# Taking the scale of W_out from the greatest upper words as loaded, on VectorE, instead of from sums of squares on ScalarE

## The chip, the cores and the metric

The kernel runs on one core of a Trainium2 chip. Its time is the device time of one execution, in microseconds (us); the median of three runs is 661.01 us (660.56 to 662.23). The profiled execution, from which all rows below come, took 662.76 us, of which 661.0 us lie between its first and its last instruction (the span).

## What is computed

Attention with a decay over 8 batches, 8 heads, 576 positions and 64 columns a head, and on its result, as 4608 tokens of 512, one layer with a gate by softmax, a normalisation and two weight matrices. All inputs are float64.

```python
scores = scale * np.matmul(q, k.transpose(0, 1, 3, 2))
decay = cum[:, :, :, None] - cum[:, :, None, :]        # cum: running sum of log f
scores = np.where(causal, -1000000000.0, scores + decay)
attn = softmax(scores)
x = (attn @ v) as [4608, 512]
h = x @ w_in                                            # [512, 1024]
solu = h * softmax(h)
ln = (solu - mu) / np.sqrt(var + 1e-06) * g_ln
out = ln @ w_out                                        # [1024, 512]
```

## The kernel before

**Tiles.** Heads go in pairs, four pairs a batch, 32 in all (p from 0 to 31). The 576 queries of a pair are cut into five tiles (i from 0 to 4; 64 rows, then four of 128), and a tile of scores is as wide as its last key: 64, 192, 320, 448, 576. The first three tiles of a pair are its first half, the last two its second. `score_products` (lines 802 to 829) makes the scores in PSUM; `scores` (831) takes on VectorE the row minima nm and moves the scores to SBUF (line 846), on ScalarE the exponential with its sums (851), on POOL the sums' last touch (857), on VectorE the reciprocal ri (858), and then scales the weights. For batch 0, whose pairs are 0 to 3, POOL scales them (the helper's line 509), TensorE transposes them (898), ScalarE or VectorE copies them out as t_p (507, 509), and the products with v are in f32 (923). Later batches split into f16 upper and lower parts and transpose by DMA (516, 928). `values` ends with x_h on ScalarE (938) and x_l on VectorE (939): upper part and remainder of a layer's input. The layer over 128 tokens at a time (36 of them) has products with W_in (959 to 961), the softmax and normalisation (970 to 1006), and products with W_out (1029 to 1031), each matrix in an upper and a lower f16 part.

**W_out.** It comes as float64 in four quarters of 1 MB into two landing buffers by turns, t_raw (in a buffer that the transposed weights of the second half use later) and vraw of batch 1. `weights` (572) makes f32 of a quarter: ScalarE takes the upper words (line 586), POOL the top bits of the lower words (589), and VectorE joins them into wo_f (591). `prepare_w_out` (724) then has ScalarE square each of the quarter's two halves, times g and a small constant, with the sum of each row going into `tops["wo"]` (735 and 736; gs, made by POOL in line 568, holds g times the constant). `scale` (634) takes the greatest of the eight columns (640), turns it with TensorE (645), makes a power of two of it (`exponents`, 648), spreads it by TensorE (670) and reads it back (675, 676). `scale_w_out` (739) multiplies g by it into sg and makes the f16 parts (744 to 753). For W_in, `scale_w_in` (625) does otherwise: VectorE takes the greatest absolute value among the upper words as loaded, read as f32 (line 629), and `exponents` undoes the shift of the exponent (653, 654).

**Order.** Every piece of work is an `op` with an engine, a length and what it reads and writes. `Plan.schedule` (115) gives each op a rank, by its number in the table `RANK` (line 97: `o.due = RANK[o.seq]`), and lets each engine take, among the ops that are ready in the plan, the one of least rank. This sets the order of all five queues, and each engine takes its queue in order on the chip. Where the plan sees TensorE idle in its first 300 us, blank products of `ident` are written into TensorE's queue to the length of the gap (lines 1142 to 1155); they write to a bank that is free and are read by nobody.

```python
def share(t):
    return next((x for a, e, x in FILLED if a <= t / 1e3 < e), 0.0)
...
idle += [(x, k, int(share(t) * (y - x) / (256 * COLUMN))) for k, x, y in plan.spare(busy + 100.0, t)]
...
nc.tensor.matmul(dst[:, :256], blank[:, :P], blank, start=True, stop=True)
```

## Time and profile before

| | |
|---|---|
| median of the runs | 661.01 us |
| profiled execution | 662.76 us, span 661.0 us |
| TensorE (PE) | 632.1 us, 96% |
| VectorE (DVE) | 553.3 us, 84% |
| ScalarE (ACT) | 513.1 us, 78% |
| POOL | 399.8 us, 60% |
| DMA | 110.80 MB, mean 168 GB/s |
| blank products (line 1154) | 131 |

An engine's share is over the whole span. Where one engine has nearly no gaps, the time is what stands in its queue plus its gaps, and a row of the order of time names for each gap what ended it. The reader should keep apart the start (to about 55 us, in which batch 0 and the weights are prepared), the long middle, and the last 40 us, in which only the layer is left.

### The profile page before, as it was taken

The page shows a single profiled execution, that of the slowest core. Times are in us where ns is not written, and L with a number is a line of the kernel's source. Part 1 is how long each engine was busy: PE and PEld are TensorE (multiplying, and loading weights), DVE is VectorE, ACT ScalarE, POOL GpSimd, SP SyncE. Part 2 cuts the span into 40 slices and gives each one's busy share as a digit, 9 for nine tenths or more (in the row PEclk, how much of TensorE's full clock was granted, in tenths as well). Part 3 has the DMA queues.
Part 4 walks back from the last instruction along what each step waited for, and adds up shares of the span by engine and source line. Part 5 has one row for each costly group of instructions (what it writes and reads, how often), then busy time and mean ns, then how long its engine had stood idle before and what let it go on. Part 6 is the DMA issues. An engine that isn't in the chain of part 4 may idle for free. (4 is left out here: it accounts for less than half of the span.)

```text
span 661.0 us, 17338 instructions
## 1 busy us (share of the span) xinstructions
PE 632.1 (96%) x6305; PEld 345.3 (52%) x6305; DVE 553.3 (84%) x1644; ACT 513.1 (78%) x1290; POOL 399.8 (60%) x625
## 2 busy tenths in 40 slices
PE   5989999999999998989989999999999899999998
PEld 4666655554545545444545545445545455544445
DVE  6967999999999999999979989899899977983122
ACT  6899848978988897788877987987688679674333
POOL 3475851477766855768666756783787544667420
PEclk8999999999999999999999999999999999999999
DMA  8846118969899998999789899999849886887341
GB/s 333 330 168 223 57 53 216 169 108 235 166 183 202 197 204 150 189 200 214 182 156 214 145 199 218 178 183 189 137 85 179 130 150 101 148 156 139 75 96 48
DMA packets 262710, 110.80 MB, mean 168 GB/s; under 512 B 248288, under 2 KB 248736, under 8 KB 261600
## 3 DMA queue, kind: packets, MB, share of 16 engines
q1 hardware_dynamic: 262624, 109.69, 79.4%
q8 instruction: 49, 0.80, 0.5%
q14 instruction: 37, 0.30, 0.1%
HBM read 38.27 MB, written 9.66 MB: 73 GB/s over the span
## 5 line engine op out<-in xcount | busy, mean ns | idle before, releaser
L851 ACT ACTIVATE p<-p,nm 128x320 f32<-128x320 f32 (+4 forms) x208 | 133.0, 641 | 22.9 <-DVE nm L846 22.5
L825 PE MATMUL ps<-qk 64*128 64x288 f16 (+9 forms) x1056 | 104.2, 305 | 11.9 <-DMA qk<-in_qk_dram 5.8
L959 PE MATMUL hps<-wi_h,x_h 128*128 128x512 f16 x288 | 109.6, 381 | 1.8 <-DVE e L977 1.6
L857 POOL TENSOR_SCALAR sm<-sm 128x2 f32<-128x2 f32 (+1 forms) x128 | 36.6, 286 | 122.6 <-ACT p L851 80.1
L961 PE MATMUL hps<-wi_h,x_l 128*128 128x512 f16 x288 | 109.1, 379 | 0.0
L960 PE MATMUL hps<-wi_l,x_h 128*128 128x512 f16 x288 | 109.1, 379 | 0.0
L1029 PE MATMUL ps<-wo_f,zz 128*128 128x512 f16 x280 | 106.6, 381 | 0.0
L1031 PE MATMUL ps<-wo_f,zz 128*128 128x512 f16 x280 | 106.1, 379 | 0.0
L1030 PE MATMUL ps<-wo_f,zz 128*128 128x512 f16 x280 | 106.1, 379 | 0.0
L846 DVE CUSTOM_DVE_ANT_0 p<-ps,mask 128x320 f32<-128x320 f32 (+4 forms) x208 | 98.2, 495 | 2.7 <-POOL unscale L696 1.0
L879 DVE SCALAR_TENSOR_TENSOR wo_p<-p,ri,wo_p 128x448 f16<-128x448 f32 (+1 forms) x112 | 91.1, 838 | 2.6 <-ACT wo_p L507 1.9
L928 PEld LDWEIGHTS <-v 128*64 128x64 f16 x2520 | 70.8, 110 | 25.5 <-issue 22.3
L928 PE MATMUL ps<-t_p,v 128*64 128x128 f16 (+1 forms) x2520 | 79.7, 219 | 4.6 <-ACT y L1061 1.6
L1001 POOL TENSOR_TENSOR z<-e,z 128x1024 f16<-128x1024 f32 x32 | 71.7, 2240 | 20.0 <-ACT z L507 19.4
L970 DVE TENSOR_REDUCE st<-hps 128x1 f32<-128x1024 f32 x36 | 43.8, 1215 | 33.6 <-PE hps L961 33.5
L509 POOL TENSOR_SCALAR wo_p<-p,ri 128x576 f16<-128x576 f32 x56 | 50.9, 915 | 15.6 <-DVE ri L858 14.1
L973 ACT ACTIVATE e<-hps,st,unscale 128x1024 f32<-128x1024 f32 x32 | 38.4, 1199 | 23.9 <-DVE st L971 17.9
L977 DVE SCALAR_TENSOR_TENSOR e<-hps,e 128x1024 f32<-128x1024 f32 x36 | 43.9, 1219 | 11.6 <-ACT e L973 11.5
L825 PEld LDWEIGHTS <-qk 64*128 64x128 f16 x864 | 32.8, 94 | 38.4 <-issue 27.0
L823 PE MATMUL ps<-crow,pick 64*128 64x448 bf16 (+1 forms) x360 | 51.8, 276 | 0.0
L987 ACT ACTIVATE junk<-e,st 128x1024 bf16<-128x1024 f32 x36 | 41.2, 1146 | 9.6 <-DVE e L977 9.5
L959 PEld LDWEIGHTS <-x_h 128*128 128x128 f16 x288 | 28.1, 97 | 37.4 <-issue 8.3
(188 smaller groups left out, 1315.7 us busy)
## 6 DMA issues: line engine op xcount, KB each, us to landing
raws<-in_qk_dram SPq DMA_DIRECT2D x24, 576.0 KB, 5.0
vraw<-in_v_dram SPq DMA_DIRECT2D x8, 1280.0 KB, 7.7
out_dram<-y SPq DMA_DIRECT2D x35, 256.0 KB, 2.9
qk<-in_qk_dram SPq DMA_DIRECT2D x8, 576.0 KB, 9.2
wo_raw<-in_w_in_dram SPq DMA_DIRECT2D x4, 1024.0 KB, 8.3
t_raw<-in_w_out_dram SPq DMA_DIRECT2D x2, 1024.0 KB, 4.9
vraw<-in_w_out_dram SPq DMA_DIRECT2D x2, 1024.0 KB, 6.3
t_p<-p16s SPq DMA_TRANSPOSE x84, 3.4
```

The costliest lines, as they stand in the source:

```text
L825: nc.tensor.matmul(dst, x[row(h), 0, q0:q0 + P], y[row(h), 1, cols], start=(n == 0), stop=False)
L846: op(DVE, R_NS[i] if n == 0 else 442, at[i][h] + STEPS[0], lambda i=i, h=h, n=n, a=a, e=e, x=x, m0=m0: nc.vector.tensor_tensor_reduce(home ...
L851: op(ACT, E_NS[i] + (0 if banked(p, i) or i == 4 else 28), at[i][h] + STEPS[1], lambda i=i, h=h, x=x: nc.scalar.activation(home(i, h), hom ...
L879: op(DVE, L_NS[j], at[j][g] + STEPS[4], lambda j=j, g=g, nq=nq, h16=h16, l16=l16, r1=r1: nc.vector.scalar_tensor_tensor(l16(), home(j, g, ...
L928: nc.tensor.matmul(o[row(h), a:a + n], v16[m][:, x, 2 * j + h], t[:, y, i + j if h else i - j], start=(j == 0 and c == 0), stop=(j == i an ...
L959: nc.tensor.matmul(hps[:, sl], x_h, wi_h[:, c, sl], start=(c == 0), stop=False)
L960: nc.tensor.matmul(hps[:, sl], x_h, wi_l[:, c, sl], start=False, stop=False)
L961: nc.tensor.matmul(hps[:, sl], x_l, wi_h[:, c, sl], start=False, stop=(c == NCC - 1))
L1001: op(Z_LO[n], {DVE: 1280, POOL: 2130}[Z_LO[n]], at, lambda: engine(Z_LO[n]).tensor_tensor(z16[:, :, 1], e2, z16[:, :, 0], ALU.subtract), [ ...
L1029: nc.tensor.matmul(o, zz[:, a, 0, j], wo(0, k), start=(k == 0), stop=False)
L1030: nc.tensor.matmul(o, zz[:, a, 0, j], wo(1, k), start=False, stop=False)
L1031: nc.tensor.matmul(o, zz[:, a, 1, j], wo(0, k), start=False, stop=(k == NFC - 1))
```

## The change

The sums of squares go, and gs with them. In their place VectorE takes, for each quarter as it was loaded, the greatest absolute value of each half's upper words, read as f32 (the values of `tops["wo"]`, two columns for a quarter). When all four are there, three small steps on 128x8 undo the exponent's shift and multiply by g, the greatest is taken by its absolute value, and `exponents` treats "wo" like "wi" from there on. The table of ranks is another one: it has 3656 numbers in place of 3660, and nearly every number differs, mostly by a few places.

```diff
-    9, 12, 5, 26, 11, 15, 13, 14, 20, 46, 23, 21, 32, 51, 30, 35, 36, 37, 39, 44, 38, 43, 47, 1, 3, 7, 4, 8, 92, 162, 149, 166, 40, 172, 19, 24, 28,
...
-    gs, sg, ones = sb("gs", NFC), sb("sg", NFC), sb("ones", P, p=1)
+    sg, ones = sb("sg", NFC), sb("ones", P, p=1)
...
-    op(POOL, 200, -20, lambda: nc.gpsimd.tensor_scalar(gs, g_sb, SMALL, 1.0, ALU.mult, ALU.mult), [("g",)], [("gs",)])
...
-        op(DVE, 160, due, lambda: nc.vector.tensor_reduce(t[:, :, NFC:], t[:, :, :n], axis=AX.X, op=ALU.max),
+        op(DVE, 160, due, lambda: nc.vector.tensor_reduce(t[:, :, NFC:], t[:, :, :n], axis=AX.X, op=ALU.max, apply_absolute_value=x == "wo"),
...
-            if x == "wi":
-                nc.vector.tensor_scalar(f, f, 2.0 ** -112, None, ALU.mult)
-                nc.vector.tensor_scalar(bits, bits, 3, None, ALU.logical_shift_left)
+            if x in ("wi", "wo"):
+                if x == "wi":
+                    nc.vector.tensor_scalar(f, f, 2.0 ** -112, None, ALU.mult)
+                    nc.vector.tensor_scalar(bits, bits, 3, None, ALU.logical_shift_left)
                 nc.vector.tensor_scalar(f, f, 2.0 ** -40, None, ALU.max)
                 nc.vector.tensor_scalar(bits, bits, 0x7F800000, None, ALU.bitwise_and)
             else:
...
-        for k in (2 * c, 2 * c + 1):
-            op(ACT, 820, due, lambda k=k: nc.scalar.activation(
-                junk[:, :DM], w()[:, (k % 2) * DM:(k % 2 + 1) * DM], AF.Square, scale=gs[:, k:k + 1], accum_out=tops["wo"][:, 0, k:k + 1]),
-               [wk, ("gs",)], [("top", "wo", k)])
+        op(DVE, 1220, due, lambda: nc.vector.tensor_reduce(
+            tops["wo"][:, 0, 2 * c:2 * c + 2], now(t).rearrange("p c n -> p (c n)").bitcast(F32).rearrange("p (k n t) -> p k n t", k=2, t=2)[:, :, :, 1],
+            axis=AX.X, op=ALU.max, apply_absolute_value=True), tk, [("top", "wo", 2 * c), ("top", "wo", 2 * c + 1)])
 
     def scale_w_out(due):
+        tw = tops["wo"][:, 0, :NFC]
+
+        def values():
+
+            nc.vector.tensor_scalar(tw, tw, 2.0 ** -112, None, ALU.mult)
+            nc.vector.tensor_scalar(tw.bitcast(I32), tw.bitcast(I32), 3, None, ALU.logical_shift_left)
+            nc.vector.tensor_tensor(tw, tw, g_sb, ALU.mult)
+        op(DVE, 300, due, values, [("g",)], [("top", "wo", k) for k in range(NFC)])
         scale("wo", "wo", 0, 1, NFC, due)
```

**VectorE's queue, between the last row minima of the first halves and the first x_l.** Names: p_63 to p_67 are the score tiles of i from 0 to 4 (the same numbers in both), nm and ri the row minima and reciprocals, t_0_raw and vraw_77 the landing buffers of W_out's quarters; L846 becomes L853, L858 L865, L591 L590, L939 L946. Before:

```order
L858 RECIPROCAL ri_89<-sm_93 128x2
L846 ISA p_63,nm_88<-ps_150,mask 128x64
...
L858 RECIPROCAL ri_92<-sm_96 128x2
L846 ISA p_67,nm_85<-ps_148,mask 128x288
...
L846 ISA p_67,nm_85<-ps_147,mask,nm_85 128x288
L846 ISA nm_85 128x1
L858 RECIPROCAL ri_92<-sm_96 128x4
L939 SCALAR_TENSOR_TENSOR x_l<-ps_145,scale_117,x_h 128x320
L591 SCALAR_TENSOR_TENSOR wo_f_669<-wo_f_669,t_0_raw 128x1024
```

Now:

```order
L734 TENSOR_REDUCE top_wo<-t_0_raw 128x2
L865 RECIPROCAL ri_89<-sm_93 128x2
...
L734 TENSOR_REDUCE top_wo<-vraw_77 128x2
L853 ISA p_67,nm_85<-ps_148,mask 128x288
...
L853 ISA p_67,nm_85<-ps_149,mask,nm_85 128x288
L853 ISA nm_85 128x1
L590 SCALAR_TENSOR_TENSOR wo_f_648<-wo_f_648,t_0_raw 128x1024
L590 SCALAR_TENSOR_TENSOR wo_f_648<-wo_f_648,vraw_77 128x1024
L946 SCALAR_TENSOR_TENSOR x_l<-ps_145,scale_116,x_h 128x320
L865 RECIPROCAL ri_92<-sm_96 128x4
```

Two of the four reductions, and the first two joins of W_out, now stand ahead of the fourth pair's reciprocal of four columns (ri_92); before, only the row minima did. The other two reductions follow: one just ahead of the last x_l, the other behind the third join.

**TensorE's queue, up to the first layer product.** L898 (now L905) are transposes of weights, L923 (now L930) products with v of batch 0, L1154 (now L1161) the blank products, L959 (now L966) the first product with W_in. Before:

```order
L898 MATMUL ps_148<-ident,p_66 128x128 x3
L1154 LDWEIGHTS ident
L1154 MATMUL ps_147<-ident 128x256
...
L898 MATMUL ps_147<-ident,p_64 128x128 x3
...
L898 MATMUL ps_146<-ident,p_63 128x64
...
L923 MATMUL ps_150<-t_1_p,vraw_76 64x64 x2
L923 MATMUL ps_150<-t_1_p,vraw_76 64x128 x10
...
L898 MATMUL ps_149<-ident,p_67 128x128 x3
L959 LDWEIGHTS x_h
L959 MATMUL hps<-wi_h,x_h 128x512
```

Now:

```order
L905 MATMUL ps_148<-ident,p_66 128x128 x3
L1161 LDWEIGHTS ident
L1161 MATMUL ps_144<-ident 128x256
...
L832 MATMUL ps_144<-qk_1_71 128x448
...
L905 MATMUL ps_147<-ident,p_63 128x64
...
L905 MATMUL ps_146<-ident,p_64 128x128 x3
L930 MATMUL ps_147<-t_1_p,vraw_76 64x64 x2
...
L930 MATMUL ps_147<-t_1_p,vraw_76 64x128 x10
...
L905 MATMUL ps_144<-ident,p_67 128x128 x3
L966 LDWEIGHTS x_h
L966 MATMUL hps<-wi_h,x_h 128x512
```

In the old piece two blank products stand where the first "..." is, then one, then ten ahead of the products with v and two behind them, and one more before the piece: 16. In the new one thirteen stand at the first "...", one ahead of the transposes of p_64, three and twelve around the products with v, and six before the piece: 35. Over the whole queue there are 151 in place of 131: 40 and 40 at the very start, 56 and 54 from there to the products of the second pair, 16 and 35 here, 19 and 22 behind. The scores of 448 columns (L832) moved from ahead of this piece into it, and three transposes of p_67 from ahead of the first layer product to behind its first two pieces.

## Rows read from the trace of the kernel before

**Rows 1.** The page, parts 1 and 2: busy time of TensorE with its share and number of instructions, and the clock granted to it in 40 slices of the span, in tenths.
```profile
PE 632.1 (96%) x6305; PEld 345.3 (52%) x6305; DVE 553.3 (84%) x1644; ACT 513.1 (78%) x1290; POOL 399.8 (60%) x625
...
PEclk8999999999999999999999999999999999999999
```

**Rows 2.** Busy time of the engines by stage: stretch, its length, then TensorE, its weight loads, VectorE, ScalarE and POOL with the number of instructions, clock, DMA share, GB/s.
```profile
40.00:50.00 10.00, 9.36 (x95) 6.36 (x94) 5.96 (x27) 9.83 (x31) 8.08 (x15) 1.00 0.59 236
50.00:60.00 10.00, 9.43 (x75) 5.86 (x76) 6.85 (x13) 8.78 (x20) 5.97 (x8) 1.00 0.62 210
60.00:70.00 10.00, 9.93 (x85) 6.13 (x82) 9.82 (x34) 9.57 (x22) 5.27 (x14) 1.00 0.53 192
```

**Rows 3.** TensorE in the order of time: start, length, engine, line, operation, tiles, shape, number of merged instructions, and in brackets the gap before it and what ended it.
```profile
50.48 0.55 PE L898 MATMUL ps<-ident,p 128*128 128x128 f32 x3 [0.43 <-POOL p L509]
...
51.49 1.27 PE L1154 MATMUL hps<-ident 128*128 128x256 bf16 x10
...
54.05 0.39 PE L1154 MATMUL ps<-ident 128*128 128x256 bf16 x2
...
55.38 0.38 PE L959 MATMUL hps<-wi_h,x_h 128*128 128x512 f16 x1
...
120.64 1.91 PE L1154 MATMUL ps<-ident 128*128 128x256 bf16 x16 [0.39 <-DVE nm L846]
```

**Rows 4.** Lines 735 and 629 by themselves (number, then shortest, median and longest in ns, first and last start), and two squares on ScalarE in the order of time.
```profile
L735 ACT ACTIVATE junk<-wo_f,gs x8: 707/720/722, 50.4 to 62.0; 128x512 bf16<-128x512 f32 x8
...
61.15 0.72 ACT L735 ACTIVATE junk<-wo_f,gs 128x512 bf16<-128x512 f32 x1
...
62.00 0.72 ACT L735 ACTIVATE junk<-wo_f,gs 128x512 bf16<-128x512 f32 x1
...
L629 DVE TENSOR_REDUCE top_wi<-wo_raw x4: 1210/1218/1220, 7.5 to 16.5; 128x1 f32<-128x1024 f32 x4
```

**Rows 5.** POOL and then ScalarE in the order of time, same stretch.
```profile
46.37 1.18 POOL L589 TENSOR_SCALAR vraw<-vraw 128x1024 int32<-128x1024 uint8 x1
...
47.92 3.31 POOL L509 TENSOR_SCALAR p<-p,ri 128x448 f32<-128x448 f32 x5
...
49.39 1.14 ACT L586 ACTIVATE wo_f<-vraw 128x1024 f32<-128x1024 f32 x1
...
54.17 0.53 ACT L938 ACTIVATE x_h<-ps,scale 128x320 f16<-128x320 f32 x1 [0.38 <-PE ps L923]
```

**Rows 6.** The chain of W_out's scale: VectorE, VectorE, and TensorE's first product with W_out, in the order of time.
```profile
63.14 0.15 DVE L640 TENSOR_REDUCE top_wo<-top_wo 128x1 f32<-128x8 f32 x1
...
68.98 0.22 DVE L741 TENSOR_SCALAR sg<-g_sb,scale_wo 128x8 f32<-128x8 f32 x1
...
81.97 0.38 PE L1029 MATMUL ps<-wo_f,zz 128*128 128x512 f16 x1
```

**Rows 7.** VectorE in the order of time, from the stretch of 40 to 56 us.
```profile
42.80 0.17 DVE L858 RECIPROCAL ri<-sm 128x2 f32<-128x2 f32 x1 [1.49 <-POOL sm L857]
...
47.86 0.18 DVE L858 RECIPROCAL ri<-sm 128x4 f32<-128x4 f32 x1 [0.98 <-POOL sm L857]
47.95 0.52 DVE L939 SCALAR_TENSOR_TENSOR x_l<-ps,scale,x_h 128x320 f16<-128x320 f32 x1
...
51.63 1.23 DVE L591 SCALAR_TENSOR_TENSOR wo_f<-wo_f,vraw 128x1024 int32<-128x1024 int32 x1
...
54.73 0.55 DVE L939 SCALAR_TENSOR_TENSOR x_l<-ps,scale,x_h 128x320 f16<-128x320 f32 x1 [1.42 <-ACT x_h L938]
```

**Rows 8.** What TensorE waited for, over the whole span: us in total, times, longest us.
```profile
PE ps L825 <- DVE nm L846: 4.2, 5, 1.9
PE ps L898 <- POOL p L509: 2.3, 5, 0.8
PE hps L959 <- DVE e L977: 1.6, 3, 1.2
PE ps L670 <- DVE scale L668: 1.6, 1, 1.6
PE ps L928 <- ACT y L1061: 1.6, 1, 1.6
```

**Rows 9.** TensorE in the order of time: the first and the last of its 15 waits after 200 us, and the three longest that VectorE released.
```profile
243.22 0.62 PE L928 MATMUL ps<-t_p,v 128*64 128x64 f16 x18 [0.65 <-DVE nm L846]
...
256.31 0.38 PE L670 MATMUL ps<-scale,ones 1*128 1x6 f32 x2 [1.59 <-DVE scale L668]
...
288.86 0.26 PE L825 MATMUL ps<-qk 64*128 64x64 f16 x6 [1.45 <-DVE nm L846]
...
518.07 0.26 PE L825 MATMUL ps<-qk 64*128 64x64 f16 x6 [1.88 <-DVE nm L846]
...
543.37 0.58 PE L825 MATMUL ps<-qk 64*128 64x320 f16 x6 [0.32 <-DVE nm L846]
```

**Rows 10.** What VectorE waited for, over the whole span: the first row.
```profile
DVE st L970 <- PE hps L961: 33.5, 10, 10.8
```

**Rows 11.** POOL and VectorE in the order of time, around 253 us.
```profile
253.35 2.13 POOL L1001 TENSOR_TENSOR z<-e,z 128x1024 f16<-128x1024 f32 x1 [1.68 <-ACT z L507]
...
253.24 0.16 DVE L660 TENSOR_SCALAR scale<-scale 1x3 f32<-1x3 f32 x1
253.43 2.06 DVE L661 TENSOR_SCALAR scale<-scale 1x3 int32<-1x3 int32 x1
```

289 rows, old and new, of the table RANK are left out of this document.

## The prediction

> **What bounds the kernel now.** I read the page's table of engines first. TensorE is busy 632.1 of 661.0 us at a granted clock that is full in all slices but the first [rows 1], so the end is set by the sum of what stands in TensorE's queue and of the gaps in it. VectorE, 84%, and ScalarE, 78%, matter where TensorE waits for them. The busy time holds work that computes nothing: 131 blank products of line 1154, which the planner puts into TensorE's queue wherever its plan has the engine idle, nearly all of them ahead of the first layer. TensorE takes its queue in order, so a blank product costs its issue time whether or not the wait it was meant for comes.
>
> Next I read the engines by stage, for the place where the squares stand. From 40 to 50 us ScalarE is busy 9.83 of 10 us and VectorE 5.96; from 50 to 60 us 8.78 and 6.85; after 60 us VectorE is full [rows 2]. So the removed work lies where ScalarE is the fuller of the two, and VectorE has 4.04 + 3.15 = 7.2 us free there. Then TensorE's own order of time for that stretch: one gap of 0.43 us at 50.48, ten blank products in 1.27 us, two more, then the first layer product at 55.38 [rows 3]. From there TensorE hardly stops until 120 us. What is lost before 55.38 is therefore a shift of everything behind it, unless a later wait takes it up.
>
> **The change part by part.** *ScalarE.* The eight squares last 0.72 us each, and follow each other by 0.85 us when nothing is between them [rows 4]: 8 x 0.85 = 6.8 us leave its queue between 50 and 63 us. The three that stand ahead of the last x_h (the f16 upper part of a layer's input, made on ScalarE) are 2.5 us of it. I cost this at nothing for the end: the last x_h waits at 54.17 for TensorE (0.38 us [rows 5]), whose products wait for the fourth pair's weights from POOL, so ScalarE's work is beside the path there.
>
> *VectorE.* Four reductions come in. The same reduction of W_in takes 1.22 us [rows 4]: 4.9 us. The three small steps on 128x8 are like the one of 0.22 us [rows 6]: 0.7 us. In the exponent two steps take the place of three: nothing. Against 5.6 us stand the 7.2 us free. The first two reductions go ahead of two reciprocals, in place of waits for POOL of 1.49 and 0.98 us [rows 7]. Of 2.44 us some 2.4 lie in these gaps at best and none at worst; I take most of it as covered.
>
> What is late next is the reciprocal of the fourth pair (ri_92 of four columns). Before, it runs at 47.86; now both conversions of W_out (line 590) stand ahead of it. The second of them waits for ScalarE's conversion of the same words, which in the old order ends at 50.5 [rows 5] and in the new one stands three places after the first. POOL's scaling of the fourth pair's weights follows that reciprocal, then transposes, values, x_h, x_l (the f16 remainder, on VectorE) and the first layer product. But POOL now scales the 448-wide tiles ahead of that point, where the old queue has one of them inside the 3.31 us [rows 5]. I take the two as even.
>
> *TensorE.* The real products are the same in number. The blank ones go from 131 to 151. Up to the scores of the first half of batch 0, none is added (40 at the start in both); the counts between there and the stretch that the order shows differ by two; from the values of the second pair to the first layer product 35 stand where 16 did; later 22 where 19 did. A run of ten takes 1.27 us, of sixteen 1.91 us [rows 3]: less the 0.27 us of the last one, 0.11 us each. So 20 x 0.11 = **+2.2 us**, of which 19 x 0.11 = 2.1 us stand ahead of 55.38. They cover waits that are there now: the 0.43 us at 50.48, where thirteen blank products and a score product now come first, and part of the 0.39 us at 120.64 [rows 3]. I credit **-0.4 us** for them.
>
> *SP and POOL.* No transfer is added. The reductions are one more reader of the two landing buffers, so the second half of W_out, and behind it v of batch 1, may go out up to 1.2 us later. The cover is the gap between W_out's scale and its first use: the greatest of the eight is taken at 63.14, the scale is there at 69.2, and the first product with W_out runs at 81.97 [rows 6] without a wait. An earlier scale earns nothing for the same reason. POOL loses one step of 0.2 us that nothing waits for.
>
> *The rest of the order.* The table of ranks is new throughout, but no engine gets other work after 90 us. The neighbours differ by one or two places on most of each queue, and in the last stage on TensorE by up to twelve. No row prices that. Its bounds are the waits that are there: besides the start, TensorE waits 4.2 us for the row minima that free a score bank, 2.3 us for POOL's weights, 1.6 us each for the scales, the layer's e and a value bank, and more below [rows 8]. In the order of time they are 15 after 200 us, 13.2 us in sum, the first at 243.22 and the last at 543.37; the 11 of them that VectorE releases make 8.6 us, with 1.88 us at 518.07, 1.59 us at 256.31 and 1.45 us at 288.86 the longest [rows 9]. A TensorE that is 1.8 us later finds such a wait shorter, if VectorE's chain there does not itself start at TensorE. It mostly does: VectorE waits 33.5 us in ten waits for TensorE's layer products [rows 10]. Between nothing and -1.8 us I take **-0.3 us**, near nothing for that reason.
>
> One wait shows how much is chance. At 253.43 a step on three numbers took 2.06 us, from 0.08 us after POOL's subtraction of 2.13 us began until it ended, and TensorE then waited 1.59 us for the scales at 256.31 [rows 9, 11]. The Trainium skill, SBUF — State Buffer, section Who interferes with whom, calls VectorE's second port pair and GpSimd's one pair that one of them holds for a whole instruction; this trace agrees. By that rule a reduction with one input, which does not run in a two-port mode, is not held up by POOL's byte steps beside it, and the four cost what I took; were they held as the 2.06 us step was, each would lose up to 1.18 us, one byte step of POOL [rows 5].
>
> *Sum.* 2.2 - 0.4 - 0.3 = +1.5 us on the profiled execution's 662.76 us, of which 661.0 are span: 664.3. The median of the runs is 661.01, 1.75 us below the profiled one, so 662.5 us there. A run of this kernel can be told from no change at about 0.3%, 2 us: below 659.0 or above 663.0.
>
> **The rivals.** *Slower by a new wait on VectorE.* The Trainium skill, VectorE: DVE Perf Modes, section Rules for kernel authors, expects a reduction at the lowest rate and advises against it on a hot path; the trace's 1.22 us for 1024 elements [rows 4] agrees on the rate. As a mechanism here: the gaps at 42.80 and 47.86 are waits for POOL, whose sums come from ScalarE. If, with both reductions and both conversions ahead of it, the fourth pair's reciprocal runs 2.4 us later than 47.86 (2 x 1.22), then POOL's scaling, the transposes and the values move by as much and the blank products no longer cover it. It decides once the reciprocal runs later than about 49.5, that is 47.86 plus the 1.6 us that the new blank products give net. Price: up to 2.4 us more, 664.9 us. For it: the 1.49 us gap is for another reciprocal, which now runs after the reduction. Against it: POOL has less ahead of it. Chance 0.27.
>
> *Faster by later waits.* The 8.6 us that TensorE waits for VectorE after 200 us [rows 8, 9] depend on single meetings such as the one with POOL's subtraction. If a new order lets half of them go, 662.5 - 4.3 = 658.2 us. Against it: orders so alike meet as many new ones; no row favours the new order. Chance 0.21.
>
> *Nothing comes of it.* The new blank products only fill waits that the old order would have had with this work, the rest evens out: 661.0 us. The work is then moved off ScalarE and nobody notices. Chance 0.1.
>
> **How the numbers follow.** My forecast has 0.42, with its own range 660.5 to 664.5: the sum without either credit is 663.2, with the whole -1.8 us 661.0, and a half to one microsecond of chance on either side. Faster by over 0.3% comes from 0.18 of the faster rival, 0.02 of the forecast and 0.02 of the rest: 0.22. Slower comes from 0.23 of the slower rival and 0.15 of the forecast: 0.38. The remaining 0.40 is no change. The range runs from 657.5 to 666.5: the faster rival with a little more than half of the waits gone, and the slower one with 1.6 us of new waits later, the size of the one at 256.31. About 2 in 10 lie outside.
>
> **What would show it.** In the profile after: blank products 151 in number at 0.11 us apart; the first layer product 1 to 2 us after 55.38; ScalarE below 9 of 10 us between 50 and 60 us and VectorE above 8; no wait of TensorE over 0.5 us between 44 and 57 us; the first product with W_out still without a wait. The slower rival would show as a gap of over 1 us ahead of the fourth pair's transposes or the first layer product, released by POOL or VectorE. The faster one would show in the list of TensorE's waits, where the sum after 200 us would fall from some 13 us to below 9. I am wrong if the first layer product comes before 55.4, or if the waits after 200 us change by more than 3 us.

## The result and the profile after

The changed kernel takes 666.93 us (median of 12 runs, 664.6 to 672.85) against 661.33 us of the kernel before beside it: ratio 1.0089, interval 1.0072 to 1.0106, so about 5.9 us slower. The range ended at 666.5 and the forecast said 662.5, so the prediction was wrong in size; among its three cases it had given no change the best chance (0.40) and slower 0.38. One run of those below, of x8, took 1266.10 us: x8's median counts it, its ratio does not. The profiled execution took 667.18 us, 665.5 of them span; before it was 662.76 and 661.0.

The page after, where it answers [rows 1]:

```profile
PE 633.9 (95%) x6325; PEld 346.9 (52%) x6325; DVE 561.3 (84%) x1650; ACT 507.3 (76%) x1274; POOL 403.5 (61%) x624
...
PEclk8999999999999999999999999999999999899999
```

TensorE has 20 more instructions, which are the additional blank products (151 in place of 131). VectorE has 8 us more work, ScalarE 5.8 us less. One slice near 580 us has a lower clock, which [rows 1] did not have. By stage, answering [rows 2] (stretch, length, TensorE, weight loads, VectorE, ScalarE, POOL, clock, DMA share, GB/s):

```profile
40.00:50.00 10.00, 7.57 (x83) 5.19 (x81) 8.21 (x25) 9.74 (x30) 8.39 (x12) 1.00 0.68 242
50.00:60.00 10.00, 9.60 (x83) 6.94 (x84) 6.57 (x14) 5.49 (x12) 6.53 (x12) 1.00 0.49 197
60.00:70.00 10.00, 10.00 (x83) 5.68 (x81) 9.16 (x30) 2.92 (x6) 3.24 (x6) 1.00 0.55 189
```

From 40 to 50 us TensorE fell from 9.36 to 7.57: 1.8 us are lost there. ScalarE is relieved after 50 us, as meant, and nothing gets shorter by it. TensorE in the order of time, answering [rows 3]:

```profile
47.51 0.77 PE L905 MATMUL ps<-ident,p 128*128 128x128 f32 x5 [0.48 <-POOL p L509]
50.21 0.98 PE L905 MATMUL ps<-ident,p 128*128 128x128 f32 x7 [1.94 <-POOL p L509]
51.03 1.58 PE L1161 MATMUL ps<-ident 128*128 128x256 bf16 x13
...
56.22 1.48 PE L1161 MATMUL ps<-ident 128*128 128x256 bf16 x12
...
58.61 0.38 PE L966 MATMUL hps<-wi_h,x_h 128*128 128x512 f16 x1
...
84.79 0.38 PE L1036 MATMUL ps<-wo_f,zz 128*128 128x512 f16 x1
...
577.83 1.62 PE L935 MATMUL ps<-t_p,v 128*64 128x128 f16 x30 [2.24 <-DMA t_p<-wo_p]
```

There is a new gap of 1.94 us at 50.21, released by POOL. The first layer product stands at 58.61, 3.23 us later than in [rows 3]; the first product with W_out has no wait, as in [rows 6]. What POOL and then VectorE did at the gap:

```profile
47.54 2.62 POOL L509 TENSOR_SCALAR p<-p,ri 128x448 f32<-128x448 f32 x1
```
```profile
47.38 1.22 DVE L590 SCALAR_TENSOR_TENSOR wo_f<-wo_f,t_raw 128x1024 int32<-128x1024 int32 x1
48.52 1.22 DVE L590 SCALAR_TENSOR_TENSOR wo_f<-wo_f,vraw 128x1024 int32<-128x1024 int32 x1
...
50.47 0.18 DVE L865 RECIPROCAL ri<-sm 128x4 f32<-128x4 f32 x1 [0.27 <-POOL sm L864]
...
54.97 1.20 DVE L734 TENSOR_REDUCE top_wo<-t_raw 128x2 f32<-128x1024 f32 x1
```

POOL's scaling of a 448-wide tile takes 2.62 us, called the hold below. It starts 0.16 us after the first join of W_out and ends at 50.16, 0.42 us after the second. The late reciprocal of my slower rival is there too, 2.6 us later than in [rows 7], but it runs after the gap has ended, and POOL's step had its own reciprocal long before. The reduction takes 1.20 us, as [rows 4] priced it. TensorE's waits behind 100 us, answering [rows 8] (us in total, times, longest):

```profile
PE ps L832 <- DVE nm L853: 3.4, 7, 1.3
PE ps L935 <- ACT y L1068: 2.7, 2, 2.0
PE ps L935 <- DMA t_p<-wo_p: 2.2, 1, 2.2
PE ps L832 <- DVE p16s L886: 1.9, 2, 1.1
PE ps L935 <- DMA t_p<-p16s: 1.7, 3, 1.1
```

Waits for transposing transfers (t_p<-wo_p, t_p<-p16s) make 3.9 us behind 100 us, where they made 2.1 before. The sum of all waits behind 100 us goes from 14.0 to 15.1 us, and after 200 us it is 12.4 us (13.2 by [rows 9]): others went as these came. The lower clock follows the wait of 2.24 us at 577.83 (same columns as [rows 2]):

```profile
576.00:578.00 2.00, 0.17 (x7) 0.16 (x7) 1.47 (x6) 2.00 (x7) 1.64 (x3) 1.00 1.22 73
578.00:580.00 2.00, 2.00 (x36) 1.65 (x33) 1.39 (x2) 1.88 (x4) 1.72 (x4) 0.52 1.17 310
580.00:582.00 2.00, 2.00 (x17) 0.92 (x12) 1.32 (x7) 0.00 (x0) 1.70 (x4) 0.63 1.12 207
```

TensorE is busy throughout, at 0.52 and 0.63 of the full level, so 2 x (0.48 + 0.37) = 1.7 us are lost.

### The profile page after: what moved, and what is told of

Its sections match the earlier page's. It is cut to its first block, busy times and chain, and to the rows that moved or that the text cites. A ratio compares the mean times of both kernels' runs of the same rounds, so it can differ in the third digit from the quotient of the medians.

```text
span 665.5 us, 17364 instructions
## 1 busy us (share of the span) xinstructions
PE 633.9 (95%) x6325; PEld 346.9 (52%) x6325; DVE 561.3 (84%) x1650; ACT 507.3 (76%) x1274; POOL 403.5 (61%) x624
## 5 line engine op out<-in xcount | busy, mean ns | idle before, releaser
L858 ACT ACTIVATE p<-p,nm 128x320 f32<-128x320 f32 (+4 forms) x208 | 132.9, 641 | 32.0 <-DVE nm L853 30.4
L832 PE MATMUL ps<-qk 64*128 64x288 f16 (+9 forms) x1056 | 104.2, 307 | 13.2 <-DMA qk<-in_qk_dram 6.2
L966 PE MATMUL hps<-wi_h,x_h 128*128 128x512 f16 x288 | 109.7, 381 | 0.4 <-DVE e L984 0.3
L853 DVE CUSTOM_DVE_ANT_0 p<-ps,mask 128x448 f32<-128x448 f32 (+4 forms) x208 | 97.8, 496 | 9.2 <-PE ps L830 4.7
L864 POOL TENSOR_SCALAR sm<-sm 128x2 f32<-128x2 f32 (+1 forms) x128 | 38.1, 298 | 102.9 <-ACT p L858 78.2
L886 DVE SCALAR_TENSOR_TENSOR wo_p<-p,ri,wo_p 128x448 f16<-128x448 f32 (+1 forms) x112 | 93.2, 857 | 1.4 <-ACT wo_p L507 1.2
L1008 POOL TENSOR_TENSOR z<-e,z 128x1024 f16<-128x1024 f32 x32 | 69.9, 2185 | 31.0 <-ACT z L507 30.4
L509 POOL TENSOR_SCALAR wo_p<-p,ri 128x576 f16<-128x576 f32 x56 | 49.0, 882 | 16.3 <-DVE ri L865 15.4
L832 PEld LDWEIGHTS <-qk 64*128 64x128 f16 x864 | 32.9, 95 | 39.4 <-issue 27.5
L966 PEld LDWEIGHTS <-x_h 128*128 128x128 f16 x288 | 28.1, 98 | 39.0 <-issue 10.6
```

Source lines behind the costliest of these rows:

```text
L832: nc.tensor.matmul(dst, x[row(h), 0, q0:q0 + P], y[row(h), 1, cols], start=(n == 0), stop=False)
L853: op(DVE, R_NS[i] if n == 0 else 442, at[i][h] + STEPS[0], lambda i=i, h=h, n=n, a=a, e=e, x=x, m0=m0: nc.vector.tensor_tensor_reduce(home ...
L858: op(ACT, E_NS[i] + (0 if banked(p, i) or i == 4 else 28), at[i][h] + STEPS[1], lambda i=i, h=h, x=x: nc.scalar.activation(home(i, h), hom ...
L886: op(DVE, L_NS[j], at[j][g] + STEPS[4], lambda j=j, g=g, nq=nq, h16=h16, l16=l16, r1=r1: nc.vector.scalar_tensor_tensor(l16(), home(j, g, ...
L966: nc.tensor.matmul(hps[:, sl], x_h, wi_h[:, c, sl], start=(c == 0), stop=False)
L1008: op(Z_LO[n], {DVE: 1280, POOL: 2130}[Z_LO[n]], at, lambda: engine(Z_LO[n]).tensor_tensor(z16[:, :, 1], e2, z16[:, :, 0], ALU.subtract), [ ...
```

## The experiments

In all of them the planner's choice is replaced by a written list of operation numbers and a written list of blank products up to the first layer, so that one operation can be moved at a time. Blank products after 100 us are still computed from the plan (of those listed before that there are 129 in the changed order, 112 in the old one).

```diff
-            for e in stale: ... best[e] = min(ready by RANK) ...; t, o = min(best)
+            o = self.ops[ORDER[len(order)]]
...
+            for _ in range(BLANKS.get(o.seq, 0)):
+                nc.tensor.matmul(hps[:, :256], blank[:, :P], blank, start=True, stop=True)
```

A layer block is the run of products with W_in for 128 tokens. A join is VectorE's step that makes f32 of a quarter of W_out, a byte step POOL's on the lower words of it, a scaling POOL's step on a tile of weights. For every profile the table gives how much later than in the first profile of before the first layer block starts (55.38 us there), then the second one (67.53 us), and how much later the span ends. The shift of the work between 20 and 40 us, where all the orders are nearly alike, is taken off, since the start varies by a microsecond. "Late" is the order behind 62 us.

| run | early work and order; late order | median us | ratio [95%] | first, second, end |
|---|---|---|---|---|
| the change | reductions, changed; changed | 666.93 | 1.0089 [1.0072, 1.0106] | +3.40, +3.11, +4.59 |
| z1 | the same once more | 666.98 | 1.0090 [1.0057, 1.0122] | +1.73, +1.68, +3.60 |
| y4 | squares, old; old (before once more) | 661.02 | 0.9985 [0.9966, 1.0004] | +0.03, -0.05, -0.64 |
| y3 | squares, old; changed | 660.94 | 0.9970 [0.9945, 0.9995] | +0.03, -0.20, -0.80 |
| x1 | reductions, old; old | 665.84 | 1.0079 [1.0056, 1.0102] | -0.21, +4.54, +3.39 |
| x2 | squares, changed; changed | 669.41 | 1.0113 [1.0083, 1.0143] | +4.54, +4.25, +7.07 |
| x3 | change, POOL's byte step moved | 667.44 | 1.0090 [1.0073, 1.0107] | +1.70, +1.79, +4.37 |
| z2 | x3 with the next byte step moved too | 667.56 | 1.0088 [1.0054, 1.0121] | +1.73, +1.47, +7.00 |
| z3 | z2 without reductions 3 and 4 | 667.39 | 1.0090 [1.0059, 1.0120] | +1.58, +1.29, +4.03 |
| x4 | change without 13 blank products | 665.85 | 1.0063 [1.0042, 1.0083] | +1.85, +1.72, +3.80 |
| x6 | reductions, changed; old | 666.43 | 1.0077 [1.0053, 1.0101] | +1.78, +2.55, +1.68 |
| y1 | x6, byte step moved, without the 13 | 666.37 | 1.0067 [1.0045, 1.0088] | +1.82, +2.59, +3.70 |
| x5 | x1, last two reductions moved | 667.13 | 1.0085 [1.0066, 1.0103] | -0.24, +3.13, +4.62 |
| x8 | old; two reductions, four squares | 664.36 | 1.0035 [1.0017, 1.0052] | +0.05, +1.55, +3.04 |
| y2 | x8, both reductions earlier | 664.11 | 1.0020 [0.9999, 1.0041] | +0.79, +0.68, +0.57 |
| x9 | x8 without 15 blank products | 667.47 | 1.0092 [1.0073, 1.0112] | +0.06, +1.86, +2.67 |
| z5 | before without the same 15 | 663.82 | 1.0038 [1.0020, 1.0056] | +0.81, +1.48, +1.68 |
| z6 | before and 19 blank products | 664.75 | 1.0050 [1.0031, 1.0069] | +2.06, +1.92, +4.68 |
| z7 | y3 and the same 19 | 665.19 | 1.0048 [1.0025, 1.0071] | +2.05, +1.58, +4.76 |

One profile's end varies by some 3 us, so the early columns are read from profiles, the cost from the ratios. Each ratio is to runs of before beside it, and these differ from set to set.

### The work or the order

x1 does the new work in the old order, each reduction behind its quarter's conversion on ScalarE or its join; x2 does the old work in the changed order.

```diff
 ORDER, VectorE's part in x1:
-  ri_92 (4 columns), x_l, join 1, ..., join 2, x_l, x_l, join 3, copies, join 4, copy
+  reduction 1, ri_92, x_l, join 1, ..., join 2, x_l, reduction 2, x_l, join 3, reduction 3, copies, join 4, reduction 4, three small steps, copy
```

> The changed work (reductions on VectorE, no squares) in the order of the kernel before: every other operation stands on its engine where it stood before the change, with the 131 blank products where they were; the first reduction stands ahead of the reciprocal of the fourth pair, the second behind the third x_l, the third and fourth behind their conversions. Theory A (the loss is one of places: two conversions of W_out one behind the other on VectorE keep POOL from its scaling, and blank products stand ahead of the scores): about 661 us, within 1.5 us of the kernel before, first layer product at 55.4 to 56.0 us, no tile of 448 columns over 2 us on POOL. Theory B (the reductions themselves cost it: 4.9 us more on VectorE before the first layer): 664 us or more, with the first layer product at least 1.2 us behind 55.38.

> The other way about: the work of the kernel before (eight squares on ScalarE, no reductions) in the order of the changed kernel, with its 151 blank products; the squares stand in ScalarE's queue behind the exponentials near 50 us and behind the last two conversions. Theory A (places): slower than before by 3 to 6 us, with a 448-wide scaling of over 2 us on POOL and a gap of 1.5 to 2 us ahead of seven transposes near 50 us. Theory B (the reductions): within 1.5 us of the kernel before.

Both are slow, which neither theory had. The changed order costs at least as much with the old work (669.4) as with the new, so it is slow without the new work. And the old order has no room for four reductions. In x1 the first layer block is on time, but between it and the second one TensorE waits for copies (TensorE, VectorE, ScalarE in the order of time):

```profile
63.92 0.55 PE L930 MATMUL ps<-t_p,vraw 128*64 128x128 f32 x6 [2.10 <-DVE t_p L509]
```
```profile
59.83 1.23 DVE L590 SCALAR_TENSOR_TENSOR wo_f<-wo_f,vraw 128x1024 int32<-128x1024 int32 x1 [0.95 <-POOL vraw L588]
60.97 1.21 DVE L734 TENSOR_REDUCE top_wo<-vraw 128x2 f32<-128x1024 f32 x1
...
62.71 1.15 DVE L509 TENSOR_SCALAR t_p<-ps 128x384 f32<-128x384 f32 x2
```
```profile
58.52 1.14 ACT L585 ACTIVATE wo_f<-vraw 128x1024 f32<-128x1024 f32 x1 [3.03 <-DMA vraw<-in_w_out_dram]
```

The copies stand behind the fourth reduction, and that behind a load of the fourth quarter which came late because the second reduction held its buffer. ScalarE, whose queue holds exponentials behind this conversion, waits 3.03 us for the same load. Behind TensorE's wait of 2.10 us the clock falls (columns as in [rows 2]):

```profile
64.00:66.00 2.00, 1.33 (x19) 0.87 (x19) 2.00 (x11) 0.85 (x3) 0.64 (x1) 0.89 0.94 333
66.00:68.00 2.00, 2.00 (x21) 1.98 (x20) 1.65 (x7) 1.67 (x4) 0.88 (x3) 0.50 1.05 426
68.00:70.00 2.00, 2.00 (x13) 1.35 (x11) 0.80 (x2) 1.96 (x5) 1.72 (x3) 0.76 0.40 160
```

That is 2 x (0.11 + 0.50 + 0.24) = 1.7 us of x1's +4.54. In x5 the third reduction stands ahead of its join and the fourth behind two more copies:

```diff
-  join 3, reduction 3, copy, copy, copy, join 4, reduction 4, small steps, copy, copy
+  reduction 3, join 3, copy, copy, copy, join 4, copy, copy, reduction 4, small steps
```

> As the run with the old order and the new work, but with the last two reductions elsewhere on VectorE: the third ahead of its conversion (it can't go behind the copies of the turned weights, which write into the buffer that it reads), the fourth and the three small steps behind the two copies that TensorE waited 2.10 us for near 63.9. Theory F (the first two reductions stand in gaps, the last two meet a VectorE that is full from 55 us on): the wait of 2.10 us falls below 1 us, the time comes down by 1 to 2 us from 665.8, to about 664.3, since the fourth reduction now holds back the load of v that uses its buffer. Theory G (the last two are no worse than the first two; the loss of that run lies in the late stages): the time stays at 665 to 666.5.

The second block stands at +3.13 instead of +4.54, and the runs gain nothing (667.1). The clock does not fall here, and the wait for the copies is 0.96 us, but TensorE now waits for the greatest of W_out's columns, which the late fourth reduction holds back:

```profile
66.36 0.27 PE L644 MATMUL ps<-ident,top_wo 128*1 128x128 f32 x1 [2.41 <-DVE top_wo L639]
```

x8 does reductions for the first two quarters alone, squares for the others, and x9 takes 15 blank products between 47 and 54 us out of it:

```diff
+        if c < 2: op(DVE, 1220, ... tensor_reduce as in the change ...)
+        for k in (2 * c, 2 * c + 1) if c > 1 else (): op(ACT, 820, ... Square ...)
...
 x9, BLANKS, ahead of the transposes and products from 47 to 54 us:
-  225: 2, 223: 1, 231: 10, 372: 2
```

> The kernel before with half of the change: the first two chunks of W_out by a reduction on VectorE each (in the two places that the run with the old order gave them, and their four greatest then multiplied by g and squared), the last two by four squares on ScalarE as before; every other operation and the blank products in the old order. Theory F: the first layer product at about 54.5 as in the run with the old order, no wait for the copies near 64 us, and 660.3, 0.9 us below the kernel before. Theory G (each reduction costs alike): 663 to 664.

> As the run with two reductions and four squares, without the 15 blank products that stand between 47 and 54 us; no work of the reference is left out. Theory C (there they are on the path of TensorE, which in the run with the old order waited for nothing between 48.4 and 58.9): the first layer product another 0.8 us earlier (1.6 us of blank products less what the weights' copies of ScalarE then make TensorE wait), 659.5. Theory D (they fill waits): no change against the run beside it.

x8 has +0.05 and +1.55: of x1's +4.54, 3.0 come with the last two reductions, 1.7 of these through the lower clock, which x8 does not have. Taking blank products out made it slower (667.5); x9's profile shows no cause for that in the start (its two blocks stand as in x8). y2 puts both reductions into earlier gaps, so that the second no longer holds the buffer:

```diff
-  row minima of p_67, reduction 1, ri_92, ..., join 2, x_l, reduction 2, small steps
+  reduction 1, row minima of p_67, reduction 2, small steps, ri_92, ..., join 2, x_l
```

> As the run with two reductions and four squares, but with the first reduction in the gap ahead of the scores near 43.4 us and the second where the first was, so that the load of the last chunk waits for a conversion only, as in the kernel before. Theory H (that run lost its 1.5 us between 55 and 66 us because the second reduction held the load of the last chunk back, and ScalarE's exponentials stand behind that chunk's conversion): the third and fourth conversion at 55.9 and 59.2 as before, no loss between 55 and 80 us, 660.5 to 662. Theory I (VectorE's 2.4 us come out anyway): 663.5 to 664.5.

The second block improves from +1.55 to +0.68, so of the 1.55 us at most 0.9 was the held load (the first reduction moved too). What is left is a wait for POOL of 0.98 us at 50.71 (0.43 us in [rows 3]). By its ratio its time, 664.1, cannot be told from before, and it is not faster.

### The pieces of the changed start

x3 moves POOL's byte step of the second quarter behind the scaling that was held; x4 takes out the 13 blank products behind the gap; x6 has the old order from 64 us on.

```diff
 x3, ORDER, POOL:
-  byte step 2, scaling 320, scaling 448
+  scaling 320, scaling 448, byte step 2
 x4, BLANKS:
-  375: 13
```

> The changed kernel with one step moved: on POOL the byte step of W_out's second chunk goes behind the two scalings (320 and 448 columns) that it stood ahead of. Nothing else. Theory A: the 448-wide scaling then runs before both conversions and takes 0.64 us in place of 2.62, the gaps of 0.48 and 1.94 us ahead of the twelve transposes go, the first layer product comes 1.5 to 2.3 us before 58.61, and the time falls by as much, to about 665. Theory C (the blank products and what stands behind them set the first layer product): the gaps go, but the first layer product moves by under 0.5 us and the time stays near 667.

> The changed kernel without the 13 blank products that stand between the seven transposes and the scores of 448 columns near 51 us; it leaves out no work of the reference. Theory C (these blank products are on the path: VectorE waited 2.27 us for those scores and POOL 2.31 us for VectorE): the scores come 1.4 us earlier, the first layer product 1.0 to 1.4 us before 58.61, the time falls by about 1.3 us to 665.5. Theory D (they fill a wait that is there anyway): a new wait of about 1.4 us stands in their place ahead of the scores, and the time stays.

> The changed kernel up to about its first layer products (order and blank products as they are there), and from there on the order of the kernel before. Theory L (the changed order of the last stages costs by itself: TensorE waited 2.24 us for the transposed weights near 578 us and lost clock behind it): about 664, the first 3.1 us lost by 80 us as in the changed kernel, no wait over 1 us for the transposed weights behind 560 us, no drop of the granted clock there. Theory M (such waits come with any shift of the ramp): 666 to 667.

In x3 the scaling is free (four tiles in 2.63 us), TensorE's gap is gone and the first block stands at +1.70 where the first profile of the change had +3.40. Yet the runs are as slow as the change. In x4 other waits came in place of the 13 products, which are 1.4 us at 0.11 us each, and the first block stands at +1.85, where it stands in the other profiles without a hold:

```profile
47.10 1.72 PE L905 MATMUL ps<-ident,p 128*128 128x128 f32 x12 [0.33 <-POOL p L509]
...
50.50 0.64 PE L832 MATMUL ps<-qk 64*128 64x448 f32 x1 [0.74 <-DVE x_l L946]
```

So the 13 cover a wait and cost the first block nothing. The time, 665.9, is 1.1 us below the change's, within the intervals of the two. x6, with the old order from 64 us on, takes 666.4: the changed late order is not what makes the change slow. y1 joins the three edits:

> The changed kernel with what the earlier runs named put right: the byte step of the second chunk behind the two scalings on POOL, the 13 blank products ahead of the 448-wide scores left out, and from about the first layer products on the order of the kernel before. The work is the changed kernel's, all four reductions included. Theory P (the loss is the port hold and the blank products in the ramp and the order of the late stages): the 448-wide scaling at 0.64 us, the first layer product at 56.0 to 56.5, under 1 us behind the kernel before by 100 us, and 661.5 to 663. Theory R (the reductions keep VectorE and the loads late whatever the order): 664 or more.

It is 666.4: what can be mended in the start by such moves is not the cost. The changed kernel was then profiled once more (z1, the change as a written list, nothing else):

> The changed kernel once more, its order written out, for a second profile of it. If the ramp's loss is a fixed thing: the 448-wide scaling held for over 2 us again, a gap of 1.5 to 2 us ahead of the seven transposes near 50 us, the second block of layer products (67.5 before) at 70.3 to 70.8, and 666 to 668. If the hold is a race that POOL sometimes wins, as in two of the runs with this ramp: no gap, the second block at 69 to 69.5.

```profile
46.72 0.64 POOL L509 TENSOR_SCALAR p<-p,ri 128x448 f32<-128x448 f32 x1
```
```profile
47.10 1.33 DVE L590 SCALAR_TENSOR_TENSOR wo_f<-wo_f,t_raw 128x1024 int32<-128x1024 int32 x1
48.35 1.21 DVE L590 SCALAR_TENSOR_TENSOR wo_f<-wo_f,vraw 128x1024 int32<-128x1024 int32 x1
```
```profile
46.69 1.71 PE L905 MATMUL ps<-ident,p 128*128 128x128 f32 x12 [0.29 <-POOL p L509]
...
56.36 0.38 PE L966 MATMUL hps<-wi_h,x_h 128*128 128x512 f16 x1
```

POOL's step starts 0.38 us before the join and takes 0.64 us; the join takes 1.33 instead of 1.22. The first block is at +1.73. Same order, other execution: the hold of the first profile is a meeting that comes or does not. In x4 and x6, whose order here is the change's, POOL starts 0.13 and 0.18 us ahead of the join, takes 0.64 us, and the join 1.59 and 1.53. z2 moves both byte steps, z3 then leaves out reductions 3 and 4 and takes the scale from the first two quarters:

```diff
 z2, ORDER, POOL:
-  byte step 2, scaling 320, scaling 448; ...; byte step 3, ..., scaling 576
+  scaling 320, scaling 448, byte step 2; ...; scaling 576, byte step 3
 z3: reductions 3 and 4 left out, the greatest taken over four columns
```

> The changed kernel with two byte steps of POOL moved behind the scalings that they stood ahead of: that of the second chunk behind the 320- and 448-wide ones (as in the run before), that of the third behind the second 576-wide one, for which the last transposes ahead of the first layer product waited. Theory S (two causes in turn: POOL's queue sets the first block of layer products, VectorE's the second): the first layer product at 55.5 to 56.3, but the second block not before 69 us, since VectorE carries the last two reductions between 54 and 62 us; 665 to 666. Theory P (POOL's queue was all): the second block at 67.5 to 68 us and 663.

> The run with both byte steps behind, and without the third and fourth reduction: W_out's scale is then taken from the first two of its four chunks alone. Theory S: VectorE is 2.4 us freer there, the second block of layer products at 67.3 to 68.0, 662.5 to 664. Rival (VectorE does not set the second block): as the run beside it.

Neither changes the first block or the time by more than the scatter: the third byte step is not on the path there, and by these runs two of the four reductions are free in the changed order, unlike in the old one.

### The late order, and a delay by itself

y3 has the start of before to 62 us and the changed order from there; y4 is before, written out.

> The kernel before, work and order, up to 62 us, and from there on the order of the changed kernel; no reduction in it. Theory L (the changed order of the late stages costs by itself): the first layer product at 55.4, nothing lost by 100 us, a wait of some 2 us for transposed weights near 575 us, and 663 to 664. Theory N (it costs nothing on average): 660.5 to 662.

> The kernel before once more, its order written out and its blank products before the first layer all into one accumulator, to have a second profile of it: 661 to 662; between two profiles of one kernel no stage should differ by more than the runs do, about 2 us. If the late stages of this profile end over 1 us sooner against the ramp than in the first profile, then single profiles tell that much less of late waits.

They take 660.9 and 661.0 us: the thousands of ranks that differ behind the start cost nothing by themselves. (y3's ratio lies just below one, but before itself, y4, came to 0.9985 beside it.) So the loss begins ahead of 62 us; but there only +1.7 us is to be seen without a hold. z6 puts 19 blank products right ahead of the first layer product of before, z7 the same into y3; z5 takes the 15 away from before.

```diff
 BLANKS, z6 and z7 (283 is the first layer product):
+  283: 19
 BLANKS, z5:
-  225: 2, 223: 1, 231: 10, 373: 2
```

> The kernel before, work and order, with 19 more blank products right ahead of its first layer product, the number that the change added there: a pure shift of TensorE by 19 x 0.108 = 2.05 us at that place. Handed on whole: first and second block 2 us later, 663.2 to 664.0. Taken up by later waits: 661 to 662. Made larger by later waits (the changed kernels ended 1 to 3 us later than their shift at 100 us): 665 to 667.

> The same 19 blank products in the run with the changed order from 62 us on. If only the changed late order makes a shift larger (that order without a shift ended at 660.9): 664.5 to 667 here, and 663 to 664 in the run beside it. If it hands it on whole: 662.5 to 663.5.

> The kernel before, with its work and order, without the 15 blank products that stand between 47 and 54 us. Theory D (they fill waits): no difference, 661 to 662, the first layer product at 55 to 55.4. Theory C: 0.8 us faster. Theory B2 (blank products are worth more than they fill; the run with two reductions lost 3 us in its median without them): 663 to 665.

z6 shows the products themselves: 19 in 2.24 us, and the layer product 2 us later.

```profile
55.27 2.24 PE L1151 MATMUL hps<-ident 128*128 128x256 bf16 x19
57.34 0.38 PE L959 MATMUL hps<-wi_h,x_h 128*128 128x512 f16 x1
```

A delay of 2.05 us costs 3.3 us of time with the old late order (0.0050, interval 2.0 to 4.6 us) and 3.2 us with the changed one (0.0048, 1.7 to 4.7 us), each against the runs of before beside it. Against y3, which was timed beside other runs of before, z7 is 4.2 us slower by the medians (665.19 - 660.94), 5.2 us by the two ratios. Each interval alone reaches down to the delay itself; the 24 runs of both, against the 23 of before beside them, give 3.3 us, 2.2 to 4.4, so the delay costs 0.2 to 2.3 us more than itself. It is not the whole cost of the change: x3, with less delay and no hold, costs 4.8 to 7.1 us.

Where the delay's cost grows can be seen in part, in profiled executions (667.34 and 667.25 us) that were 2.6 and 2.1 us slower than the medians of z6 and z7. TensorE's waits behind 100 us in z7 and then in y3:

```profile
PE ps L1029 <- DMA zz<-z: 3.6, 2, 3.1
...
PE ps L928 <- DMA t_p<-wo_p: 2.3, 1, 2.3
...
PE ps L928 <- DMA t_p<-p16s: 1.5, 2, 1.3
```
```profile
PE ps L928 <- DMA t_p<-wo_p: 2.5, 1, 2.5
PE ps L928 <- DMA t_p<-p16s: 1.4, 2, 0.8
```

The wait for zz (the layer's normalised result, transposed on its way) is new. SP's queue in z7 and in y3, and TensorE in z7, there:

```profile
324.82 5.69 SPq L516 DMA_TRANSPOSE t_p<-p16s  x1
330.60 3.72 SPq L516 DMA_TRANSPOSE zz<-z  x1
```
```profile
322.84 3.13 SPq L516 DMA_TRANSPOSE t_p<-p16s  x1
326.06 4.79 SPq L516 DMA_TRANSPOSE zz<-z  x1
```
```profile
339.17 0.39 PE L1029 MATMUL ps<-wo_f,zz 128*128 128x512 f16 x1 [3.07 <-DMA zz<-z]
```

The transfers start 2 us apart in the two runs, as the delay has it, but the first occupies SP's queue for 5.69 instead of 3.13 us; zz goes out 4.54 us later, and TensorE waits 3.07 us. Being late does not decide this by itself: the same transfer starts later still in the first profile of the change, and in x3 (in this order), and takes less in one and more in the other.

```profile
329.76 2.49 SPq L516 DMA_TRANSPOSE t_p<-p16s  x1
```
```profile
327.24 6.06 SPq L516 DMA_TRANSPOSE t_p<-p16s  x1
```

Summed over the three kinds of transposing transfers, TensorE waits behind 100 us for 2.1 us in before, 1.7 in y4, 3.9 in y3 and in the change, 6.2 in z1, 6.3 in x4, 6.6 in x2, 7.3 in x3, 7.4 in z2, z3 and z7; with the old late order and a late start between 1.6 (y1) and 3.9 (x6). These waits go with the changed late order, which costs nothing in y3, as much as with the delay. All of TensorE's waits behind 100 us together rise less: from 14.4 us in y3 to 16.1 in z7, and from 12.2 in y4 to 13.8 in z6. What sets the length of such a transfer was not found, and that these waits make the cost of the delay is not shown.

z5 shows what blank products can be worth. Without 15 of them, 15 x 0.11 = 1.7 us, waits of 0.63, 0.25, 0.31 and 1.03 us stand in their place, and the clock falls (columns as in [rows 2], then TensorE):

```profile
54.00:56.00 2.00, 1.52 (x8) 1.52 (x9) 0.60 (x2) 1.69 (x3) 1.56 (x2) 0.65 0.95 295
56.00:58.00 2.00, 2.00 (x7) 0.93 (x6) 1.89 (x3) 1.33 (x5) 0.01 (x1) 0.50 0.55 229
```
```profile
54.48 2.11 PE L898 MATMUL ps<-ident,p 128*128 128x128 f32 x9 [1.03 <-POOL p L509]
...
56.38 0.63 PE L959 MATMUL hps<-wi_h,x_h 128*128 128x512 f16 x1
```

Layer products last 0.63 us there instead of 0.38, and the kernel is 2.5 us slower (1.0038) than with them. No version with any of the change beats the kernel before; y3 cannot be told from y4.

## Why the prediction was wrong

**Blank products, +2.2 less 0.4: the number came, its account did not.** Without the hold the first layer block is 1.6 to 1.85 us late in seven profiles (z1, x3, x4, x6, y1, z2, z3); the terms ahead of it, 2.1 less 0.4, make 1.7. But x4 and y1 lack 13 of the blank products, 1.4 us, and the block stands at +1.85 and +1.82 there all the same. So 13 of the 19 more that I counted as cost fill a wait that is there without them, and my 0.4 us for covered waits was too little. That the sum met 1.7 was luck; what makes the start that late without a hold was not found. My "no wait over 0.5 us between 44 and 57" holds in z1 and fails in the first profile.

**ScalarE at nothing: right.** It has 5.49 of 10 us where it had 8.78, and no product comes earlier.

**VectorE, "against 5.6 us stand the 7.2 us free": right only of the order that was shipped.** z3 against z2 prices the last two reductions there at nothing, within the scatter. In the old order 3.0 us at the second block come with them (x1 against x8), 1.7 of these by the clock that fell behind the wait: the free time lies ahead of 56 us, their data land later, and after 60 us VectorE is full. I added up free time without asking when the data are there. VectorE above 8 of 10 us between 50 and 60 was wrong (6.57): both joins, which I knew to stand ahead of ri_92, had moved ahead of 50 us.

**"I take the two as even": wrong in some executions.** POOL did scale the 448-wide tiles earlier, but beside two joins in a row. A VectorE step and a POOL step had met in [rows 11], with 2.06 us for a step on three numbers; I weighed such a meeting only for the reductions. The reductions met no trouble: in every profile each took 1.20 to 1.24 us, the one at 54.97 with 1.20 us beside a scaling of 0.76 us on POOL. The joins held POOL's step: 2.62 us in place of 0.64. The Trainium skill, SBUF — State Buffer, section Who interferes with whom, describes the second port pair as an exclusive lock between VectorE and GpSimd; the trace agrees, and I should have asked it of every instruction whose neighbours moved. The slower rival's sign was seen (a gap over 1 us released by POOL), its mechanism not: the late reciprocal released nothing. The hold adds 1.7 us to the first block where it comes (first profile against z1), and taking the chance of it away (x3) left the time at 1.0090, so it is not the main loss.

**SP, "the cover is the gap between W_out's scale and its first use": incomplete.** The loads of the later quarters also gate ScalarE's conversions, and exponentials stand behind these: 3.03 us of wait in x1, up to 0.9 us at the second block (y2 against x8). And the scale has a small product of its own in TensorE's queue, long ahead of that first use, which waited 2.41 us in x5. In the changed order joins and reductions come earlier, and nothing of it is seen in the first profile.

**"A TensorE that is later finds such a wait shorter", -0.3: the step that failed.** I bounded the effect of the rest of the order by nothing and -1.8 us, with no end above nothing. By the medians the change is 5.6 us slower, of which some 1.7 is the start. In x3, z2 and z3, without the hold, the start is 1.6 to 1.8 us late and the whole costs 5.8 to 6.0 us: the term was some +4 us.

The runs show a part of that. The changed late order by itself costs nothing (y3). A delay by itself is not taken up but grows: 2.05 us became 3.3 (2.2 to 4.4) in z6 and z7. My argument held only the waits that were there and none that a delay would make: the waits for zz in z7 are new, and all waits behind 100 us rise by 1.7 us from y3 to z7. The remaining some 3 us of the +4 are shown by no run: they come with the changed start (x3's 4.8 to 7.1 us lie just above z7's 1.7 to 4.7), beyond what TensorE's delay at its first two blocks shows. The clock is no answer that can be told from chance: over all runs the time lost to a lower clock, by each run's granted clock, is on average 4.7 us in before and 5.5 us in the changed kernel, a difference of 0.75 with an interval of 0.8 either way, and it is 4.4 and 4.7 us in z6 and z7 against 5.0 beside them.

None of my two signs of being wrong came: the first layer product was later than 55.4, and the waits after 200 us changed by 0.8 us in the first profile (12.4 against 13.2; 13.3 in z1). They looked at the sum of the waits, and the loss did not show there.

What stays open: why the start is 1.7 us late without a hold, what makes the larger part of the +4 us, what sets the length of the late transfers, and why x9 is slower than x8.

## What to carry to other kernels

Do not take it that later waits swallow a delay at the head of a long chain: here 2.05 us cost 3.3 (2.2 to 4.4). One kernel with some filler in front and nothing else changed tells its price, and tells also, as here, how much of a loss the delay does not explain. A term whose number comes true is not shown by that: here the sum of the blank products met the start, and taking 13 of them out showed that these cost nothing there. When an order changes, look not only at the instructions that are new but at every pair of old ones that become neighbours on engines that share something. And free time counts only from the moment the data are there.

## What the runs showed of the hardware

Two back-to-back two-input instructions on VectorE held a POOL step that began behind the start of the first: 0.64 us became 2.62 in the first profile of the change (0.16 us behind the join), and in x2 0.54 us became 2.44 (0.43 us behind), after which TensorE waited 2.20 us. Where POOL began first, it took its 0.64 us and the join took longer than its 1.22: 1.33 in z1 (POOL 0.38 us ahead), 1.53 in x6 (0.18) and 1.59 in x4 (0.13). POOL's steps and the joins stand in the same order in these five.

Behind 50 us most profiles have a stretch at the lower clock level, at changing places: 577.8 us in the change, 576 in z1, 257 in y4, 505 in y3. Each costs about 1.7 us. Of the 20 profiles four have none (before, x4, x6, x8), and x5, z2, z6 and z7 have two. Outside z5 each stands behind a wait of 1.4 to 3.1 us; but the wait of 1.88 us at 518.07 in before and one of 2.55 us at 578.35 in x4 have no fall behind them.

The issue of one transposing transfer, the same at the same place of the order, occupied SP's queue for 2.49 us in the first profile of the change, 3.13 in y3, 3.54 in z1, 5.69 in z7 and 6.06 in x3.
